# Turning batch 1's query tiles 2 to 4 by DMA, and loading batch 3 behind batch 2's x

## The chip, the core and the metric

The kernel runs on one core of a Trainium2 chip. The metric is device time in microseconds (us), median of several executions. A core has TensorE (PE; PEld is its weight load, which overlaps: 320.1 and 168.3 us busy in the 329.0 us of the kernel before), VectorE (DVE), ScalarE (ACT), GpSimd (POOL) and SyncE (SP), which here only issues DMAs, in the traces one after another (in the changed kernel a load went out at 49.41 us, when the 7.18 us turn before it had ended at 49.31): its "queue". Lines that begin with PE, DVE or the like are views of a profile; L153 is line 153 of the kernel.

## The reference

Linear attention per batch and head, then a gated feed-forward over all 4608 tokens:

```python
# attention: B=8, H=8, S=576, D=64
q_p = phi(q, cos_w, sin_w)       # relu(x)*cos | relu(x)*sin: 128 features
k_p = phi(k, cos_w, sin_w)
kv  = einsum('bhsf,bhsd->bhfd', k_p, v);  z = sum(k_p, axis=2)
x   = einsum('bhsf,bhfd->bhsd', q_p, kv) / (einsum('bhsf,bhf->bhs', q_p, z) + 1e-6)
# feed-forward: 512 -> 1536 -> 512
out = (gelu(x @ w_gate) * (x @ w_val)) @ w_out
```

## The kernel before

Tokens are handled in nine blocks: block 0 is batch 0 (576 tokens), then eight of at most 512. In a block, each of 12 units makes one 128-row slice of the gate and of the value (four matmuls each) and multiplies them. Work for other stages is hung behind units by number: `put(u, ...)` runs behind unit u. Batch b = n+1 gets its attention inside block n: scale q (`sq`) and k (`sk`), cast v, `attn_step` 0 (keys times values), then steps 1 to 5: one 128-query tile each, normalized and turned into `xT`, which later blocks multiply.

Two ways to turn a tile: TensorE transposes into a PSUM bank plus an eviction, or a DMA on SP's queue.

```python
def turn_q(b, j0, j1):                      # by DMA, SP's queue
    nc.sync.dma_start_transpose(out=qT[b % 2][:, j0:j1]..., in_=qp[:, j0:j1]...)

def q_by_pe(b, j, bank, eng, ...):          # by TensorE: 8 transposes, one eviction
    for h in range(h0, h1):
        nc.tensor.transpose(out=qb[:, h, :], in_=qp[:, j, h, :], identity=ident)
    ...
def attn_step(b, i):
    if i == 0:
        kv_half(b, 0, 6); kv_half(b, 1, 7)  # 40 short matmuls, reads kp and vx
    else:
        turn_x(b, i - 1, numer(b, i - 1, 6))    # numerators, normalize, turn x by DMA
# --- batch 1's queries, inside block 0: turned by TensorE
between = { (8, 0): (L(sq, 0, 0, "v"), L(sq, 0, 1, "s")), ...
    (9, 0): (..., L(T, 0, 6, "v")),  (9, 1): (..., L(T, 1, 7, "v")),
    (10, 0): (..., L(T, 2, 6, "v")), (10, 1): (L(load_q, 2), L(T, 3, 7, "v")),
    (11, 0): (L(T, 4, 6, "v"),), ... }
# --- end of batch 1, between output matmuls: batch 2's queries are scaled here
    x_by_pe(1, 0, y[0], 0, "s")
    o_part(0, 2, 4, 8, 12)
    sq(0, 1, "s"), sq(1, 1, "s")
    x_by_pe(1, 1, y[1], 1, "s")
    ...
# --- block 1 differs from later blocks: everything two units (attention: one) earlier
    s = 0 if n > 1 else -2
    put(4 + s, L(cast_v, b, 0, 4), L(cast_v, b, 4, 8, "s"))
    put(5 + (n == 1) + s, L(attn_step, b, 0))
    ...
```

## Time and profile before

| | before |
|---|---|
| time, median | 330.74 us (four runs, 330.67 to 330.81) |
| span of the profiled run | 329.0 us |
| PE busy | 320.1 us |
| VectorE / ScalarE busy | 172.4 / 152.3 us |
| start of block 1, of block 2 | 61.75, 85.79 us |

The page of the kernel before: busy time of each engine with its share and instruction count, and the chain of work that ended last, by engine.

```profile
PE 320.1 (97%) x2247; PEld 168.3 (51%) x2247; DVE 172.4 (52%) x381; ACT 152.3 (46%) x273; POOL 21.4 (7%) x41
...
PE 92%; DMA 3%; DVE 2%; ACT 1%; issue 1%; POOL 0%; SPq 0%; DVEq 0%; POOLq 0%; ACTq 0%
```

TensorE bounds the kernel: a microsecond counts only if it is taken from TensorE's work or from a gap in it. The gaps are few. The view of waits (engine, line, what it waited for: us in total, times, longest):

```profile
PEld L153 <- issue: 2.0, 7, 0.4
...
PE ps L169 <- ACT xT L345: 0.4, 1, 0.4
PE ps L217 <- DMA xT<-xb: 0.3, 1, 0.3
...
PE ps L342 <- DVE xb L184: 0.3, 1, 0.3
```

The last three are at 59.4, 85.8 and 25.4 us. The chain in order of time (start, us, what), one group of query transposes and the stretch before 59.4 us:

```profile
44.04 0.45 PE ps L323 x8
...
57.52 0.28 ACT qp L136
57.80 0.34 issue
58.15 0.71 ACT qp L136
58.85 0.48 ACT xT L345
59.34 0.04 issue
59.38 0.29 PE ps L169 x4
```

Eight transposes hold the chain 0.45 us. Before 59.38 us TensorE stands behind ScalarE: an eviction of x (L345) that queued behind two scalings of the next batch's queries (L136).

### The profile page before, as it was taken

How to read it: one execution, taken by the hardware profiler on the slowest of the kernel's cores; microseconds unless marked ns; L12 is line 12 of the kernel's file. 1: busy time of each engine (PE TensorE's matmuls, PEld its weight loads, DVE VectorE, ACT ScalarE, POOL GpSimd, SP SyncE). 2: the span in 40 equal slices, each digit the busy share in tenths (PEclk: the TensorE clock that was granted, in tenths of full speed). 3: DMA queues.
4: the chain of work that ended last, by engine and by line, in shares of the span. 5: the costliest groups of instructions: out<-in, count | busy, mean ns of one | idle time of the engine just before them, and what ended most of it. 6: DMA issues, size and time to landing. Idle time of an engine off the chain costs nothing.

```text
span 329.0 us, 5914 instructions
## 1 busy us (share of the span) xinstructions
PE 320.1 (97%) x2247; PEld 168.3 (51%) x2247; DVE 172.4 (52%) x381; ACT 152.3 (46%) x273; POOL 21.4 (7%) x41
## 2 busy tenths in 40 slices
PE   7799999999999999999999999999999999999994
PEld 3487876455445444544454445444544444444443
DVE  5895685668654657454835484557545322222210
ACT  6574665872564246523752376227622233222321
POOL 2650010000100010000100010001000100100000
PEclk9999999999999999999999999999999999999999
DMA  7999998799398936996599549974825121000024
GB/s 225 283 205 275 200 364 268 218 223 347 69 170 281 287 65 129 268 286 119 106 272 295 126 88 230 354 115 81 160 48 82 28 52 34 32 32 34 32 65 96
DMA packets 84635, 54.64 MB, mean 166 GB/s; under 512 B 49408, under 2 KB 79872, under 8 KB 84608
## 3 DMA queue, kind: packets, MB, share of 16 engines
q1 hardware_dynamic: 78096, 47.92, 58.8%
q0 software_dynamic: 6080, 5.90, 10.0%
q10 hardware_dynamic: 432, 0.46, 0.4%
q8 instruction: 17, 0.28, 0.3%
q14 instruction: 10, 0.08, 0.1%
HBM read 37.75 MB, written 9.44 MB: 143 GB/s over the span
## 4 chain that ended last, share of the span: by engine, by line
PE 92%; DMA 3%; DVE 2%; ACT 1%; issue 1%; POOL 0%; SPq 0%; DVEq 0%; POOLq 0%; ACTq 0%
PE ps L217 28%; PE ps L228 28%; PE ps L258 27%; PE ps L153 3%; PE ps L169 3%; DMA qf<-in_q_dram 2%; PE ps L323 1%; DMA xT<-xb 1%; PE ps L276 1%; PE ps L342 1%; ACT qp L136 0%; DVE vx L140 0%; DVE xb L184 0%; SPq L79 0%; DVE hT L233 0%
## 5 line engine op out<-in xcount | busy, mean ns | idle before, releaser
L233 DVE TENSOR_TENSOR hT<-gel,ps 128x512 bf16<-128x512 f32 (+5 forms) x126 | 76.3, 610 | 129.4 <-PE ps L228 125.8
L217 PE MATMUL ps<-xT,wg_sb 128*128 128x512 bf16 (+5 forms) x504 | 113.7, 348 | 0.8 <-DMA xT<-xb 0.3
L228 PE MATMUL ps<-xT,wv_sb 128*128 128x512 bf16 (+5 forms) x504 | 113.6, 349 | 0.0
L222 ACT ACTIVATE gel<-ps 128x512 f32<-128x512 f32 (+5 forms) x126 | 67.4, 537 | 78.0 <-PE ps L217 76.7
L258 PE MATMUL ps<-wo_sb,hT 128*128 128x512 bf16 x420 | 96.5, 379 | 0.0
L228 PEld LDWEIGHTS <-wv_sb 128*128 128x128 bf16 x504 | 47.8, 98 | 46.0
L217 PEld LDWEIGHTS <-wg_sb 128*128 128x128 bf16 x504 | 45.6, 98 | 41.1 <-issue 1.6
L258 PEld LDWEIGHTS <-hT 128*128 128x128 bf16 x420 | 40.0, 98 | 45.4
L287 ACT COPY o_sb<-ps 128x512 f32<-128x512 f32 x35 | 20.5, 585 | 74.6 <-PE ps L258 74.6
L184 DVE TENSOR_TENSOR xb<-ps,rec 128x512 bf16<-128x512 f32 (+2 forms) x41 | 27.8, 678 | 2.9 <-DMA xT<-xb 1.5
L136 ACT ACTIVATE kp<-kf,sin_c 128x512 bf16<-128x512 f32 (+1 forms) x41 | 25.4, 682 | 0.8 <-DMA kf<-in_k_dram 0.8
L134 DVE TENSOR_SCALAR qp<-qf,cos_c 128x512 bf16<-128x512 f32 x40 | 19.9, 540 | 0.0
L136 ACT ACTIVATE qp<-qf,sin_c 128x512 bf16<-128x512 f32 x29 | 19.8, 714 | 0.0
L169 PEld LDWEIGHTS <-qT 128*128 128x128 bf16 (+1 forms) x320 | 15.0, 98 | 9.1 <-issue 2.1
L134 DVE TENSOR_SCALAR kp<-kf,cos_c 128x512 bf16<-128x512 f32 (+1 forms) x45 | 18.7, 464 | 1.4 <-DMA kf<-in_k_dram 1.4
L169 PE MATMUL ps<-kv,qT 128*128 128x65 bf16 (+1 forms) x320 | 16.7, 193 | 0.5 <-ACT xT L345 0.4
L208 POOL COPY xT<-xr 128x256 bf16<-128x256 bf16 x6 | 2.7, 443 | 201.8 <-DMA xr<-xb 169.2
L153 PEld LDWEIGHTS <-kp 128*128 128x128 bf16 x320 | 10.8, 97 | 3.3 <-issue 2.0
L126 PE MATMUL ps<-junk 128*128 128x512 bf16 x35 | 10.0, 428 | 1.7 <-DVE par_i L103 1.7
L153 PE MATMUL ps<-vx,kp 128*128 128x65 bf16 x320 | 11.1, 193 | 0.1
L140 ACT CAST vx<-vf 128x1280 bf16<-128x1280 f32 (+1 forms) x9 | 10.2, 1136 | 1.2 <-DMA vf<-in_v_dram 1.2
L244 POOL COPY hT<-hT 128x768 bf16<-128x768 bf16 x8 | 7.6, 945 | 37.9 <-DVE hT L233 37.9
(56 smaller groups left out, 93.2 us busy)
## 6 DMA issues: line engine op xcount, KB each, us to landing
out_dram<-o_sb SPq DMA_DIRECT2D x38, 128.0 KB, 2.4
kf<-in_k_dram SPq DMA_DIRECT2D x7, 640.0 KB, 6.9
out_dram<-o_sb SPq DMA_DIRECT2D x16, 256.0 KB, 2.8
qf<-in_q_dram SPq DMA_DIRECT2D x6, 640.0 KB, 6.0
vf<-in_v_dram SPq DMA_DIRECT2D x6, 640.0 KB, 9.6
kf<-in_k_dram SPq DMA_DIRECT2D x7, 512.0 KB, 5.9
qf<-in_q_dram SPq DMA_DIRECT2D x6, 512.0 KB, 5.0
vf<-in_v_dram SPq DMA_DIRECT2D x6, 512.0 KB, 8.5
```

The costliest lines, as they stand in the source:

```text
L134: nc.vector.tensor_scalar(d, s, col, 0.0, op0=ALU.mult, op1=ALU.max)
L136: nc.scalar.activation(d, s, AF.Relu, scale=col)
L140: cp(vx[b % 2][:, :, h0:h1, 0:D], vf[:, h0:h1].rearrange("p h j d -> p j h d"))
L153: nc.tensor.matmul(ps[:, bank, (h % 4) * (D + 1):(h % 4 + 1) * (D + 1)], lhsT=kp[:, j, h, :], rhs=vx[b % 2][:, j, h, 0:D + 1], start=(j == ...
L169: nc.tensor.matmul(ps[0:rows, bank + g, (h % 4) * (D + 1):(h % 4 + 1) * (D + 1)], lhsT=qT[b % 2][:, t, h, 0:rows], rhs=kv[b % 2][:, h, 0:D ...
L184: nc.vector.tensor_tensor(xb[0:rows, g0:g1], nd[:, :, :, 0:D], rec[0:rows, 0:n, :, None].to_broadcast([rows, n, 4, D]), op=ALU.mult,)
L217: nc.tensor.matmul(ps[:, gb, 0:w], lhsT=wg_sb[:, ct, jt * 128:(jt + 1) * 128], rhs=xT[:, ct, p0:p0 + w], start=(ct == 0), stop=(ct == CT - 1),
L222: nc.scalar.activation(gel[:, 0:w], ps[:, gb, 0:w], AF.Gelu)
L228: nc.tensor.matmul(ps[:, vb, 0:w], lhsT=wv_sb[:, ct, jt * 128:(jt + 1) * 128], rhs=xT[:, ct, p0:p0 + w], start=(ct == 0), stop=(ct == CT - 1),
L233: nc.vector.tensor_mul(hT[n % 2][:, jt, 64 + c0:64 + c0 + w], gel[:, 0:w], ps[:, vb, 0:w])
L258: nc.tensor.matmul(ps[:, bank, :], lhsT=hT[n % 2][:, jt, c0:c0 + 128], rhs=wo_sb[:, jt, :], start=(jt == 0), stop=(jt == JT - 1),)
L287: nc.scalar.copy(o_sb, ps[:, bank, :])
```

## The change

The intent: take 24 transposes from TensorE; free batch 1's end of batch 2's scaling; keep batch 3's loads out of the way of batch 2's x; let block 1 have the same plan as later blocks. The core of the diff:

```diff
-    def x_by_pe(b, t, xb, bank, eng, c0=0, c1=CT):
+    def x_by_pe(b, t, xb, bank, eng, c0=0, c1=CT, every=1):
...
+    gv_unit(0, 1, 384, 128, 5, 7)
     X(4, 0, "v")()
-    gv_unit(0, 1, 384, 128, 5, 7)
+    gv_unit(0, 4, *A, 3, 1)
...
-        (9, 0): (L(sq, 2, 0, "v"), L(sq, 2, 1, "s"), L(T, 0, 6, "v")),
-        ... T 1 to 4 behind (9,1), (10,0), (10,1), (11,0)
+        (8, 0): (L(sq, 2, 0, "v"), L(sq, 2, 1, "s"), L(T, 0, 6, "v"), ),
+        (8, 1): (L(sq, 3, 0, "v"), L(sq, 3, 1, "s"), L(T, 1, 7, "v"), ),
+        (9, 0): (L(sq, 4, 0, "v"), L(sq, 4, 1, "s"), ),
+        (9, 1): (L(turn_q, 1, 2, 5), ),
+        (10, 1): (L(load_q, 2), ),
...
-    sq(0, 1, "s"), sq(1, 1, "s")
     x_by_pe(1, 1, y[1], 1, "s")
...
-    sq(2, 0, "v"), ... turn_q(2, 0, 3) ... turn_q(2, 3, 5)
-    load_q(3)
...                                      # blocks 1 to 6, now without the shift s:
+        put(0, ... sq 0, 1);  put(1, ... sq 2 to 4, turn_q);  put(2, 3, ... sk)
+        put(3, ..., L(cast_v, b, 0, 4))          # was unit 4 (+ s)
+        put(4, L(cast_v, b, 4, 8, "s"))
+        put(5, L(attn_step, b, 0))               # block 1: was unit 4
+            for f, u in zip((load_q, load_k, load_v), (3, 4, 5) if n > 1 else (6, 11, 11)):
+                put(u, L(f, b + 1))
+            put(6 + i, L(attn_step, b, i + 1))   # block 1: was 5 + i
```

In blocks 2 to 6, VectorE's half of the cast of v moves from unit 4 to unit 3 (in block 1, with its shift of two units, from unit 2 to unit 3). Two more edits are not in this cut: tile 4 of batch 1 is now multiplied and turned with 128 rows and not with 64 (`numer(1, 4, 0)`, `every=2`), and of batch 1's v VectorE casts heads 4 and 5 too.

More of the change, by code (lines that the diff above doesn't have):

```diff
@@ L338, in x_by_pe @@
         xb2 = xb.rearrange("p g h d -> p (g h d)")
-        rows = 128 if t < NJ else 64
+        rows = 128 if t < NJ or every == 2 else 64
         view = ps[:, bank, 0:256].bitcast(BF16).rearrange("p (c t) -> p c t", c=CT)
@@ L344, in x_by_pe @@
             )
-        cp(xT[:, c0:c1, p0:p0 + rows], view[:, c0:c1, 0:rows])
+        cp(xT[:, c0:c1, p0:p0 + rows // every], view[:, c0:c1, 0:rows:every])
     def sq(j, which, eng, *h):
@@ L454 @@
     between = {
-        (8, 0): (L(sq, 0, 0, "v"), L(sq, 0, 1, "s")),
-        (8, 1): (L(sq, 1, 0, "v"), L(sq, 1, 1, "s")),
-        (9, 0): (L(sq, 2, 0, "v"), L(sq, 2, 1, "s"), L(T, 0, 6, "v")),
-        (9, 1): (L(sq, 3, 0, "v"), L(sq, 3, 1, "s"), L(T, 1, 7, "v")),
-        (10, 0): (L(sq, 4, 0, "v"), L(sq, 4, 1, "s"), L(T, 2, 6, "v")),
-        (10, 1): (L(load_q, 2), L(T, 3, 7, "v")),
-        (11, 0): (L(T, 4, 6, "v"),),
-        (11, 1): (L(carry, 0),),
+        (7, 0): (L(sq, 0, 0, "v"), L(sq, 0, 1, "s"), ),
+        (7, 1): (L(sq, 1, 0, "v"), L(sq, 1, 1, "s"), ),
+        (8, 0): (L(sq, 2, 0, "v"), L(sq, 2, 1, "s"), L(T, 0, 6, "v"), ),
[3 more added lines that the diff above has]
+        (10, 1): (L(load_q, 2), ),
+        (11, 1): (L(carry, 0), ),
     }
@@ L465 @@
         for i, (c0, w) in enumerate((A, Bw)):
-            gv_unit(0, jt, c0, w, i, 3 - i)
+            if (jt, i) != (4, 0):
+                gv_unit(0, jt, c0, w, i, 3 - i)
             for f in between.get((jt, i), ()):
@@ L476 @@
     cast_v(1, 0, 4, "v")
-    cast_v(1, 4, 8, "s")
+    cast_v(1, 4, 6, "v")
+    cast_v(1, 6, 8, "s")
     load_v(2)
@@ L501 @@
     x_by_pe(1, 2, y[2], 6, "s")
-    y4 = numer(1, 4, 0, 64)
+    y4 = numer(1, 4, 0)
     o_part(0, 3, 5, 5, 10)
     x_by_pe(1, 3, y[3], 7, "s")
-    sq(0, 0, "v"), sq(1, 0, "v")
     o_part(0, 3, 5, 10, 12)
-    x_by_pe(1, 4, y4, 6, "s")
-    sq(2, 0, "v"), sq(2, 1, "s")
-    turn_q(2, 0, 3)
-    sq(3, 0, "v"), sq(3, 1, "s"), sq(4, 0, "v"), sq(4, 1, "s")
-    turn_q(2, 3, 5)
-    load_q(3)
+    x_by_pe(1, 4, y4, 6, "v", every=2)
     def attn_step(b, i):
@@ L529, in put @@
             a[u].extend(fs)
-        if n > 1:
-            put(0, L(sq, 0, 0, "v"), L(sq, 1, 0, "v"), L(sq, 1, 1, "v"), L(sq, 0, 1, "s"))
-            put(1, L(sq, 2, 0, "v"), L(sq, 2, 1, "s"), L(turn_q, b, 0, 3))
-            put(1, L(sq, 3, 0, "v"), L(sq, 4, 0, "v"), L(sq, 4, 1, "v"), L(sq, 3, 1, "s"), L(turn_q, b, 3, 5))
-        s = 0 if n > 1 else -2
-        put(2 + s, L(sk, 0, 0, "v"), L(sk, 1, 0, "v"), L(sk, 0, 1, "s"), L(sk, 1, 1, "s"))
-        put(3 + s, L(sk, 2, 0, "v"), L(sk, 3, 0, "v"), L(sk, 4, 0, "v"))
-        put(3 + s, L(sk, 2, 1, "s"), L(sk, 3, 1, "s"), L(sk, 4, 1, "s"))
-        put(4 + s, L(cast_v, b, 0, 4), L(cast_v, b, 4, 8, "s"))
-        put(5 + (n == 1) + s, L(attn_step, b, 0))
+        put(0, L(sq, 0, 0, "v"), L(sq, 1, 0, "v"), L(sq, 1, 1, "v"), L(sq, 0, 1, "s"))
+        put(1, L(sq, 2, 0, "v"), L(sq, 2, 1, "s"), L(turn_q, b, 0, 3))
+        put(1, L(sq, 3, 0, "v"), L(sq, 4, 0, "v"), L(sq, 4, 1, "v"), L(sq, 3, 1, "s"), L(turn_q, b, 3, 5))
+        put(2, L(sk, 0, 0, "v"), L(sk, 1, 0, "v"), L(sk, 0, 1, "s"), L(sk, 1, 1, "s"))
+        put(3, L(sk, 2, 0, "v"), L(sk, 3, 0, "v"), L(sk, 4, 0, "v"))
+        put(3, L(sk, 2, 1, "s"), L(sk, 3, 1, "s"), L(sk, 4, 1, "s"), L(cast_v, b, 0, 4))
+        put(4, L(cast_v, b, 4, 8, "s"))
+        put(5, L(attn_step, b, 0))
         if b + 1 < B:
-            if n > 1:
-                put(3, L(load_q, b + 1))
-            put(4 + s, L(load_k, b + 1))
-            put(5 + s, L(load_v, b + 1))
+            for f, u in zip((load_q, load_k, load_v), (3, 4, 5) if n > 1 else (6, 11, 11)):
+                put(u, L(f, b + 1))
         for i in range(5):
-            put(6 + (n == 1) + s + i, L(attn_step, b, i + 1))
+            put(6 + i, L(attn_step, b, i + 1))
     for n in range(2, NB):
```

## The prediction

> **What bounds it now.** TensorE: on the page PE is busy 320.1 of 329.0 us, VectorE 52%, ScalarE 46%. The chain that ended last is 92% PE; from 90 us on its PE pieces touch (four 512-column matmuls every 0.86 us). Only PE work taken away, or PE gaps closed, counts. PE's listed waits after the start are short: 0.3 to 0.4 us each at 25.4 (tile 4's x of batch 0), 59.4 (ScalarE's eviction of x) and 85.8 us (DMA of batch 2's x).
>
> **Step 1, query turns of batch 1.** Each group of 8 TensorE transposes holds the chain for 0.45 us (39.65 to 46 us, no PE gap around). Three go: -1.33 us, all critical. VectorE loses three evictions of 0.68 us, worth nothing by themselves. [...] here a 24-block turn took 5.8 us to land. It is off the path if in time: v of batch 1 is issued at 39.5 to 42.2 and lands by 48.6, so the turn should land near 50; its first reader runs near 54. Queries landed by 34.1; first use moves to about 35.
>
> **Step 2, batch 2's query scaling moved from batch 1's end into block 1.** Two ScalarE scalings (0.66 us each) stand before the eviction of x that PE waits for at 59.4. The chain there spends 2.65 us on about 2.1 us of PE work: -0.5 us. Tile 4 with 128 rows costs up to 0.1 us. Later blocks already scale this way without a gap.
>
> **Step 3, start of batch 0.** The 128-column unit put before tile 4's transposes covers the gap at 25.4, but its value needs a bank that VectorE frees at about 25.6: 0.1 us won. With (4, first half) moved ahead, unit (4, second half) follows unit (1, 64 columns) on the same two banks: PE waits for a Gelu, about 0.2 us. Together about +0.1 us.
>
> **Step 4, batch 3's loads behind batch 2's x.** Now 3.5 MB of loads are in flight when batch 2's x is turned: tiles 0 to 3 land in 8.7, 7.0, 5.2, 3.1 us; in quiet blocks 2.4 to 2.5. But attention moves one unit later (about 2 us), and block 2 needs tile 3 at once. From its numerator: 1.9 us to normalized x, 2.5 landing, 0.2 overhead = 4.6 us, against 4.0 us of PE work: a gap of about 0.6 where 0.4 is now, +0.2 us. Keys of batch 3 land an estimated 7.5 to 8.5 us into block 2, needed from 7.6: a short wait, hidden by two banks.
>
> **Total.** -1.33 - 0.5 + 0.1 + 0.1 + 0.2 = about -1.4 us: 329.3 us, range 328.4 to 330.4. Faster by over 2% 0.01, within 2% 0.98, slower 0.01.
>
> **What would show it.** 24 PE transposes fewer and 1.3 us less from 39 to 46 us; no PE wait on the DMA into qT; the PE wait at 59 us gone; a short PE wait on a Gelu near 28 us; a PE wait of 0.3 to 0.9 us on the DMA into xT at block 2's start, tile 3 landing in about 2.5 us; blocks 3 to 8 unchanged to 0.1 us.
>
> **What would make it wrong.** The turn of batch 1's queries landing after its numerators: a stall of some us. Keys or values of batch 3 over 3 us late: a stall in block 2. A later tile 3: up to 1.5 us more. Batch 1's keys or values, now needed 1.4 us earlier, not there yet.

## The result

| | before | after |
|---|---|---|
| time, median (range) | 330.74 us (330.67 to 330.81) | 328.77 us (328.19 to 329.17) |
| span of the profiled run | 329.0 us | 326.8 us |
| PE busy, matmuls | 320.1 us, 2247 | 317.6 us, 2223 |

The ratio is 0.9939 (95% interval 0.9922 to 0.9956): the mean time of one kernel's fast runs over that of the other's of the same rounds, so not quite the ratio of the medians. In us it is -2.0, inside the stated range but 0.6 more gain than the -1.4 predicted.

Where the time went, from the starts of TensorE's matmuls in the two profiles, counted from the first gate matmul. That matmul itself starts between 15.6 and 16.2 us in profiles whose program is the same up to there, so the start is left out.

| stretch | before | after | difference | predicted |
|---|---|---|---|---|
| first gate to first output matmul (block 0) | 30.64 | 29.58 | -1.06 | -1.33 + 0.1 |
| to block 1 (end of batch 1) | 15.02 | 14.29 | -0.73 | -0.5 + 0.1 |
| to block 2 (block 1) | 24.04 | 24.34 | +0.30 | +0.2 |
| to the last matmul (blocks 2 to 8) | 238.75 | 238.20 | -0.55 | 0 |

The 0.1 in the first row is step 3, that in the second row step 2's tile 4 with 128 rows.

The waits of the kernel after, same view:

```profile
PEld L153 <- issue: 0.7, 2, 0.4
...
PE ps L217 <- DMA xT<-xb: 0.8, 1, 0.8
...
PE ps L228 <- DVE hT L233: 0.2, 1, 0.2
...
PE ps L217 <- ACT gel L222: 0.2, 1, 0.2
```

The wait for ScalarE's eviction (L169) is gone. The wait for batch 2's x has grown from 0.3 to 0.8 us. The two 0.2 us waits are new, at 25.2 and 29.6 us, in block 0. And the unnamed wait at L153 fell from 2.0 to 0.7 us.

That last line holds the surprise. The chain, before and then after, in block 2:

```profile
99.76 0.86 PE ps L217 x4
100.62 0.86 PE ps L228 x4
101.49 1.36 PE ps L153 x40
```

```profile
97.95 0.86 PE ps L217 x4
98.81 0.86 PE ps L228 x4
99.67 1.21 PE ps L153 x40
```

The same 40 matmuls hold the chain 0.15 us less, and so they do in each of blocks 2 to 6. VectorE's timeline (start, us, engine, line, operation) around them, before and then after:

```profile
99.87 0.69 DVE L233 TENSOR_TENSOR hT<-gel,ps 128x512 bf16<-128x512 f32 x1 [2.44 <-PE ps L228]
100.47 0.95 DVE L140 CAST vx<-vf 128x1280 bf16<-128x1280 f32 x1
```

```profile
95.53 0.95 DVE L140 CAST vx<-vf 128x1280 bf16<-128x1280 f32 x1
98.05 0.69 DVE L233 TENSOR_TENSOR hT<-gel,ps 128x512 bf16<-128x512 f32 x1 [1.57 <-PE ps L228]
```

Before, the cast of v ended at 101.42 us (100.47 + 0.95), and the matmuls that read it could start only then; after, it ends 3 us ahead of them. That is one theory. The rival, a guess that no view shows: TensorE's program is 24 matmuls shorter, so instruction fetch falls elsewhere; "issue" is the profile's word for a wait without a visible cause.

SP's queue, before and then after, at the turn of batch 1's queries:

```profile
39.46 2.72 SPq L79 DMA_DIRECT2D vf<-in_v_dram  x4
42.34 1.83 SPq L79 DMA_DIRECT2D qf<-in_q_dram  x2
```

```profile
39.41 2.62 SPq L79 DMA_DIRECT2D vf<-in_v_dram  x4
42.13 7.18 SPq L144 DMA_TRANSPOSE qT<-qp  x1
49.41 1.32 SPq L79 DMA_DIRECT2D qf<-in_q_dram  x2
```

The turn holds the queue for 7.18 us, and batch 2's query load goes out 7 us later than before. Inside the whole change nobody needs those queries until block 1.

### The profile page after: what moved, and what is told of

It is laid out like the page before. It is cut to its first block, busy times and chain, and to the rows that moved or that the text cites. A ratio compares the mean times of both kernels' runs of the same rounds, so it can differ in the third digit from the quotient of the medians.

```text
span 326.8 us, 5867 instructions
## 1 busy us (share of the span) xinstructions
PE 317.6 (97%) x2223; PEld 167.0 (51%) x2223; DVE 171.8 (53%) x382; ACT 150.6 (46%) x270; POOL 21.2 (6%) x41
## 4 chain that ended last, share of the span: by engine, by line
PE 93%; DMA 3%; DVE 1%; ACT 1%; issue 1%; POOL 0%; SPq 0%; DVEq 0%; POOLq 0%; ACTq 0%
PE ps L217 28%; PE ps L228 28%; PE ps L258 28%; PE ps L169 3%; PE ps L153 3%; DMA qf<-in_q_dram 2%; PE ps L323 1%; DMA xT<-xb 1%; PE ps L342 1%; PE ps L276 1%; DVE vx L140 0%; SPq L79 0%; DVE hT L233 0%; DVE qT L331 0%; DVE xb L184 0%
## 5 line engine op out<-in xcount | busy, mean ns | idle before, releaser
L169 PEld LDWEIGHTS <-qT 128*128 128x128 bf16 (+1 forms) x320 | 15.0, 98 | 8.7 <-issue 1.9
L136 ACT ACTIVATE qp<-qf,sin_c 128x512 bf16<-128x512 f32 x27 | 18.5, 712 | 0.0
L169 PE MATMUL ps<-kv,qT 128*128 128x65 bf16 (+1 forms) x320 | 16.5, 193 | 0.2
L153 PEld LDWEIGHTS <-kp 128*128 128x128 bf16 x320 | 10.9, 97 | 2.6 <-issue 0.7
L153 PE MATMUL ps<-vx,kp 128*128 128x65 bf16 x320 | 11.1, 193 | 0.1
```

The source lines that it names most:

```text
L136: nc.scalar.activation(d, s, AF.Relu, scale=col)
L153: nc.tensor.matmul(ps[:, bank, (h % 4) * (D + 1):(h % 4 + 1) * (D + 1)], lhsT=kp[:, j, h, :], rhs=vx[b % 2][:, j, h, 0:D + 1], start=(j == ...
L169: nc.tensor.matmul(ps[0:rows, bank + g, (h % 4) * (D + 1):(h % 4 + 1) * (D + 1)], lhsT=qT[b % 2][:, t, h, 0:rows], rhs=kv[b % 2][:, h, 0:D ...
```

## The experiments

Twelve kernels ran; all gave the correct result. Each was timed beside the kernel before on its chip.

| run | us, median | before there | ratio |
|---|---|---|---|
| cast_only | 329.94 | 330.58 | 0.9984 |
| turn_only | 333.82 | 330.58 | 1.0092 |
| act_only | 330.18 | 330.58 | 0.9986 |
| after_rep | 328.81 | 330.58 | 0.9948 |
| turn_back | 330.13 | 331.04 | 0.9977 |
| cast_back | 330.06 | 331.04 | 0.9979 |
| x_pe | 328.35 | 331.04 | 0.9924 |
| loads_early | 334.08 | 331.04 | 1.0105 |
| q_first | 335.07 | 330.63 | 1.0124 |
| bank_free | 328.66 | 330.63 | 0.9933 |
| best1 | 327.95 | 330.63 | 0.9918 |
| best2 | 327.52 | 330.63 | 0.9904 |

### The cast of v: cast_only and cast_back

To the kernel before (cast_only):

```diff
-        put(4 + s, L(cast_v, b, 0, 4), L(cast_v, b, 4, 8, "s"))
+        put((3 if n > 1 else 4) + s, L(cast_v, b, 0, 4))
+        put(4 + s, L(cast_v, b, 4, 8, "s"))
```

> The kernel before with one line moved: in blocks 2 to 6 VectorE casts heads 0 to 3 of v after unit 3 and not after unit 4. TensorE's program is not changed by a single instruction. Theory (the cast ended 0.05 us before the keys-times-values matmuls could start, so they started 0.15 us late in five blocks): the 0.37 us between the last value matmul and the second weight load of those matmuls falls to 0.22 us in blocks 2 to 6 and the time falls by 5 x 0.15 = 0.77 us, to about 330.0. Rival (the 0.15 us per block is instruction fetch, and left because TensorE's program is 48 instructions shorter): nothing changes, 330.7.

Measured: -0.64 us by the medians, -0.53 us by the ratio (95% interval -0.96 to -0.13). In the profile the time from the last value matmul to the second weight load of the 40 is 0.37 us before and 0.22 us here, in all five blocks, and from block 2 to the last matmul the program takes 238.00 us against 238.75: five times 0.15. The chain in block 2, to be held against the 1.36 us of the kernel before:

```profile
101.21 1.21 PE ps L153 x40
```

TensorE's program is unchanged, so the rival falls.

The reverse, to the changed kernel (cast_back):

```diff
-        put(3, ..., L(cast_v, b, 0, 4))
-        put(4, L(cast_v, b, 4, 8, "s"))
+        put(3, ...)
+        put(4, L(cast_v, b, 0, 4), L(cast_v, b, 4, 8, "s"))
```

> The changed kernel with VectorE's cast of v heads 0 to 3 after unit 4 again in blocks 1 to 6; nothing else. Theory: +0.15 us in each of five or six blocks, +0.8 us, about 329.6, and the 0.37 us before the second weight load of the keys-times-values matmuls is back. Rival (that gap came from where TensorE's program is fetched): no change, 0.22 us stays.

Measured: 330.06 us; against the changed kernel, by the ratios to before (0.9979 here), +1.0 to +1.3 us (0.9948 or 0.9939), with two chips between them. The profile shows the mechanism more sharply than the times: 0.37 us is back in five blocks, and from block 2 to the last matmul the program takes 238.95 us against 238.20 in the changed kernel, +0.75 = 5 x 0.15. In block 1 the first of the matmuls came 0.47 us later than with the early cast, but block 2's wait for x was 0.4 us shorter in exchange.

### The turn by DMA: turn_only, turn_back, q_first

turn_only is the kernel before with the new table `between` and tile 4 of batch 1 turned with 128 rows (`every=2`), nothing else.

> The kernel before with query tiles 2 to 4 of batch 1 turned by DMA (queries scaled one unit pair earlier, tile 4's x turned with 128 rows), nothing else. Theory: 24 transposes of TensorE are gone, 3 x 0.445 = 1.33 us on the path, and the next stage is still TensorE's: about 329.4. Rival (the next stage is held by ScalarE and VectorE, whose casts of v end just before the keys-times-values matmuls, so part of the gain turns into a wait there): 0.3 to 0.8 us less gain, 329.7 to 330.2, with a gap before the first of those matmuls.

Measured: 333.82 us, 3.2 us slower than before. Both expectations missed the time. Their first step held: block 0 is 1.35 us shorter than before. The stretches behind it lost more: 1.0 us at the end of batch 1, 1.9 us in block 1, 1.9 us in blocks 2 to 8 (by the profiled run, one of the slower ones). The two matmuls that ended a wait in its TensorE timeline there, and SP's and ScalarE's side of the first:

```profile
58.89 0.29 PE L169 MATMUL ps<-kv,qT 128*128 128x65 bf16 x4 [1.59 <-ACT xT L345]
87.12 1.04 PE L217 MATMUL ps<-xT,wg_sb 128*128 128x512 bf16 x4 [2.28 <-DMA xT<-xb]
```

```profile
42.01 6.53 SPq L144 DMA_TRANSPOSE qT<-qp  x1
48.63 1.32 SPq L79 DMA_DIRECT2D qf<-in_q_dram  x2
...
57.04 1.33 ACT L136 ACTIVATE qp<-qf,sin_c 128x512 bf16<-128x512 f32 x2 [1.02 <-DMA qf<-in_q_dram]
58.27 1.05 ACT L345 COPY xT<-ps 128x512 bf16<-128x512 bf16 x2
```

Batch 2's queries landed at 57 us, because their load stood behind the turn. ScalarE waited for them, the eviction of x waited for ScalarE, and TensorE for the eviction: 1.59 us. A second wait of 2.28 us came at block 2's start. There is a third loss behind it, in the chain:

```profile
87.12 1.04 PE ps L217 x4
88.16 1.48 PE ps L228 x4
```

Four matmuls that take 0.86 us in the kernel before took 1.48: TensorE's clock was granted at half for 3.41 us from 88.27 us on (a mean of 0.78 from 86 to 90 us and of 0.79 from 90 to 94). In the six executions the mean clock of the span was 0.993 to 0.995 in the four slowest (333.48 to 335.12 us) and 1.000 in the two fastest (331.81 and 332.28).

The fall came after the wait: TensorE had been idle for 2.28 us up to 87.12 us and at work again for 1.15 us when the clock fell at 88.27. In q_first below, the granted clock was 0.77 from 86 to 90 us and 0.81 from 90 to 94, after a wait of 2.01 us; in loads_early, with a wait of 4.56 us, it was at half for 6.83 us (a mean of 0.51 and 0.64 in the same two windows). In the changed kernel, with its wait of 0.85 us, it was 1.00 from 75 to 325 us. What sets the fall off was not tested.

The opposite experiment turns tiles 2 to 4 on TensorE again within the changed kernel (turn_back):

```diff
-        (9, 0): (..., L(sq, 4, 1, "s"), ),
-        (9, 1): (L(turn_q, 1, 2, 5), ),
+        (9, 0): (..., L(sq, 4, 1, "s"), L(T, 2, 6, "v"), ),
+        (9, 1): (L(T, 3, 7, "v"), ),
+        (10, 0): (L(T, 4, 6, "v"), ),
...
-    y4 = numer(1, 4, 0)
+    y4 = numer(1, 4, 0, 64)
...
-    x_by_pe(1, 4, y4, 6, "v", every=2)
+    x_by_pe(1, 4, y4, 6, "v")
```

> The changed kernel with query tiles 2 to 4 of batch 1 turned by TensorE again; the rest of the change stays. Theory (inside the whole change the DMA turn is free, because batch 2's queries, whose load stands behind it in the DMA queue for 7 us, are no longer needed before block 1): +1.33 us, about 330.1, with the stretch from unit (7,0) to the first output matmul 1.33 us longer. Rival (the DMA turn also costs something inside the whole change, through the late query load): under 0.9 us more.

Measured: 330.13 us, +1.0 to +1.3 us over the changed kernel by the ratios, whose job was another. In the profile block 0 is 1.36 us longer, as the theory says; block 2's wait for x is 0.42 us instead of 0.85, so a part comes back, as the rival says. From the first gate to the last matmul it is +1.25 us. That includes 0.22 us at the end of batch 1 from tile 4, which this run turns with 64 rows again (see act_only). So the same turn is worth 1.0 to 1.3 us inside the change, while turn_only lost 3.2 us with it. One thing that differs is who needs the queries that stand behind it: that accounts for the loss at the end of batch 1, not for the larger one from block 2's start on.

q_first tests the loss at the end of batch 1 by order: turn_only with the query load ahead of the turn.

```diff
-        (9, 1): (L(turn_q, 1, 2, 5), ),
-        (10, 1): (L(load_q, 2), ),
+        (9, 1): (L(load_q, 2), L(turn_q, 1, 2, 5), ),
```

> The kernel before with batch 1's query tiles 2 to 4 turned by DMA, as in the run turn_only (333.8 us), but with the load of batch 2's queries issued ahead of that turn and not behind it. Theory (turn_only lost because the turn holds the DMA queue 6.5 us and batch 2's queries then land at 57 us, after ScalarE wants them): the queries land by about 50, the 1.6 us wait of TensorE for ScalarE's eviction falls back to 0.35 us or less, and the time is at least 1.2 us below turn_only: 330 to 332.5, lower if the wait at block 2's start (2.3 us there) goes too. Rival (the turn itself, or its lateness for tiles 2 to 4, is what costs): a wait on the DMA into qT appears and the time stays near 333.8.

Measured: 335.07 us, no better, as the rival says. Its TensorE waits after block 0:

```profile
55.24 0.43 PE L169 MATMUL ps<-kv,qT 128*128 128x65 bf16 x8 [1.38 <-DMA qT<-qp]
59.13 0.29 PE L169 MATMUL ps<-kv,qT 128*128 128x65 bf16 x4 [0.47 <-ACT xT L345]
87.10 1.04 PE L217 MATMUL ps<-xT,wg_sb 128*128 128x512 bf16 x4 [2.01 <-DMA xT<-xb]
```

The mechanism of the theory held: with the queries in time, the wait for ScalarE fell from 1.59 to 0.47 us. But its time did not: the turn now landed 11.6 us after its issue and was itself waited for, 1.38 us. In neither order were both in time. With the early need for the queries taken away, as in the change, the turn fits; other ways were not tried.

The wait at block 2's start stayed at 2.0 to 2.3 us in both kernels. The lateness of batch 3's loads does not look like the cause: their query load left SP's queue at 69.6 to 69.9 us, where it left at 69.0 before, but the last of them landed at 83.6 to 83.7 us, as before (83.75). Tiles 1 to 3 of x landed 1.4 us later than before all the same. The DMA packets in the traces show a candidate that no run tested. The page lists a queue q8, "instruction" (17 packets, 0.28 MB in the kernel before); one 16 KB transfer on it ran from 83.6 to 84.8 us in turn_only and from 84.0 to 85.1 in q_first, where it ran from 79.5 to 80.6 before. Then the DMA all but stopped while three turns of x were under way, in turn_only (the last two figures are DMA share and GB/s):

```profile
84.30:85.50 1.20, 0.55 (x3) 0.05 (x1) 1.20 (x3) 0.32 (x1) 0.00 (x0) 1.00 0.06 6
```

The changed kernel shows the same in small: of its first three turns of batch 2's x two landed in 2.5 to 2.7 us, and the third, into which such a transfer fell (80.1 to 81.5 us), in 4.2.

### The scaling behind the eviction: act_only

To the kernel before:

```diff
-    sq(0, 1, "s"), sq(1, 1, "s")
     x_by_pe(1, 1, y[1], 1, "s")
...
     x_by_pe(1, 2, y[2], 6, "s")
+    sq(0, 1, "s"), sq(1, 1, "s")
```

> The kernel before with the two ScalarE scalings of batch 2's queries tiles 0 and 1 put behind the eviction of x of tile 2 and not before that of tile 1; nothing else. Theory: the eviction of tile 1 is no longer behind 1.3 us of scaling, TensorE's wait at 59.4 us is gone: -0.6 us, 330.1. Rival (the wait only moves to the eviction of tile 3, which then stands behind the same scalings): under 0.2 us of gain.

Measured: -0.40 us by the medians, -0.46 by the ratio (95% interval -0.89 to -0.03). The wait at 59.4 us is gone from the profile, and block 1 starts 0.51 us earlier, counted from the first gate. The rival falls. The change gets 0.73 us in this stretch, and the profiles tell where the other 0.22 us come from: tile 4 of batch 1 with 128 rows. turn_back, which has the 64 rows and everything else of this stretch as the change, takes 14.51 us for it, as act_only does, against 14.29. Tile 4's eight numerators in the chain, here (64 rows) and in the changed kernel (128 rows):

```profile
58.77 0.37 PE ps L169 x8
```

```profile
57.40 0.26 PE ps L169 x8
```

The other half of the 0.22 us lies around the tile's four transposes. The prediction had booked the 128 rows as a cost of up to 0.1 us.

### The loads behind batch 2's x: loads_early

To the changed kernel:

```diff
-            for f, u in zip((load_q, load_k, load_v), (3, 4, 5) if n > 1 else (6, 11, 11)):
+            for f, u in zip((load_q, load_k, load_v), (3, 4, 5)):
```

> The changed kernel with batch 3's loads where all later blocks have them (q, k, v after units 3, 4, 5 of block 1) and not behind batch 2's x. Theory (loads in flight slow the turns of x): tile 0's turn lands in 5 us or more instead of 2.5, tile 3's later too, and block 2's wait grows from 0.9 us by 0.5 to 1.2 us: 329.3 to 330.0. Rival (the loads are over by the time tile 3 is turned; the wait is the turn's own latency): no change, within 0.2 us.

Measured: 334.08 us, about 5.3 us slower than the changed kernel (328.81) by the medians of two jobs; the direction was right, the size not. From issue to landing (min, median, max) of the four turns of x by DMA, in the changed kernel and in this one:

```profile
DMA to landing us min/median/max: 2.5/2.8/4.2
```

```profile
DMA to landing us min/median/max: 4.8/6.7/10.1
```

SP's queue backed up behind the first turns, tile 3 was issued at 83.0 us and took 4.8 us, and TensorE stood still. Timeline, chain, and a window with the granted clock (after the engines' busy times: clock, DMA share, GB/s):

```profile
87.85 1.89 PE L217 MATMUL ps<-xT,wg_sb 128*128 128x512 bf16 x4 [4.56 <-DMA xT<-xb]
...
87.85 1.89 PE ps L217 x4
89.73 1.71 PE ps L228 x4
...
86.00:90.00 4.00, 2.15 (x6) 0.78 (x7) 1.28 (x2) 0.23 (x1) 0.38 (x2) 0.51 0.55 104
```

The wait is 4.56 us against 0.85, and then four matmuls take 1.89 and 1.71 us, about twice the 1.02 and 0.86 us of the kernel before, at a granted clock of 0.51. So putting batch 3's loads behind batch 2's x is not a nicety: without it the change would lose 3 us to the kernel before. How much of the 4.56 us is the loads alone was not separated: an instruction transfer of 16 KB ran here too, from 83.3 to 84.9 us, amid the turns. That moving the attention one unit later needs the loads' new place, and the moved scaling the later attention, is argued, not tested.

### The rest: x_pe, bank_free, best1, best2, after_rep

x_pe takes the remaining wait of block 2 (0.85 us) by turning one tile of x on TensorE, whose transposes fit behind the next tile's numerators:

```diff
+        elif (b, i) == (2, 4):
+            held.append(numer(b, 3, 6))
         else:
             turn_x(b, i - 1, numer(b, i - 1, 6))
+            if (b, i) == (2, 5):
+                x_by_pe(2, 3, held[0], 4, "s")
```

> The changed kernel with tile 3 of batch 2's x turned by four TensorE transposes and a ScalarE eviction instead of a DMA; nothing else. Theory (the 0.85 to 0.98 us in which block 2's first matmul waits is the latency of that one tile's DMA): the wait goes, 0.22 us of transposes come: -0.6 to -0.75 us, about 328.1. Rival (tile 2's DMA, or the DMA queue in general, is as late): the wait shrinks by less than 0.4 us, 328.6 or more.

Measured: 328.35 us, ratio 0.9924 against 0.9939 and 0.9948 of the changed kernel, so -0.5 to -0.8 us. The wait is gone; the transposes hold the chain 0.22 us. The theory holds.

bank_free changes the banks of one unit in block 0:

```diff
-                gv_unit(0, jt, c0, w, i, 3 - i)
+                gv_unit(0, jt, c0, w, *((4, 6) if (jt, i) == (4, 1) else (i, 3 - i)))
```

> The changed kernel with unit (4, second half) of batch 0 on banks 4 and 6 and not on banks 1 and 2, which the unit before it has just filled; nothing else. Theory (TensorE waits 0.20 us for that unit's Gelu): the wait at 29.6 us goes, -0.2 us, 328.6. Rival (the wait moves to the next unit): no change.

Measured: 328.66 us. The times can't tell 0.2 us apart. In the profile the wait for the Gelu is gone and block 0 is 0.37 us shorter than in the changed kernel.

best1 joins x_pe and bank_free:

> The changed kernel with tile 3 of batch 2's x turned by TensorE (as x_pe, 328.35) and unit (4, second half) on free banks (as bank_free). Theory: the two gains add, 328.1 to 328.2, and TensorE has no listed wait over 0.3 us after 26 us. Rival: one of them hides the other, 328.35 or more.

Measured: 327.95 us. The gains add, and in the same job it is 0.7 us below bank_free.

best2 adds to best1:

```diff
-    gv_unit(0, 1, 384, 128, 5, 7)
-    X(4, 0, "v")()
-    gv_unit(0, 4, *A, 3, 1)
+    gv_unit(0, 4, *A, 1, 3)
+    X(4, 0, "s")()
+    gv_unit(0, 1, 384, 128, 5, 7)
```

> best1 with unit (4, first half) put ahead of tile 4's transposes and of the 128-column unit, and tile 4 evicted by ScalarE. Theory: the longer unit (0.87 us) covers the wait for tile 4's normalized x and for VectorE's bank at 25.2 us: another -0.25 us, about 327.9. Rival (its value weights, which landed only near 25.5 us in the kernel before, are now waited for): a wait on the DMA into wv_sb and no gain.

Measured: 327.52 us, the fastest of all: ratio 0.9904 to the kernel before. No wait on the weights appears, and the wait at 25.2 us is gone. By the two ratios it is about 1.1 to 1.5 us faster than the changed kernel.

after_rep is the changed kernel again:

> The changed kernel once more, unchanged. Its four runs spread over 1.0 us (328.2 to 329.2) where the kernel before spreads over 0.14. Theory: a wait for a DMA at the start of block 2 varies between executions: again a spread of about 1 us, and the wait on the DMA into xT in the profile differs from 0.85 us. Rival: the first job's spread was chance, and runs now agree within 0.2 us.

Measured: 328.81 us, 328.46 to 329.21; the wait on the DMA into xT was 0.98 us. But the kernel before spread as much on this chip (330.12 to 331.12), so the narrow 0.14 us of its first runs says nothing special; neither the theory of the varying wait nor an agreement within 0.2 us is borne out.

## Why the prediction was right or wrong

The total was right, 328.77 us in a range of 328.4 to 330.4, with 0.6 us more gain than the point. That it came so near the range's lower end is owed to gains that the prediction did not have, the cast of v (0.75 us) and tile 4's rows (0.22 us), against a little less than predicted in blocks 0 and 1. Point by point:

- **What bounds it: right.** Every effect found is TensorE work or a TensorE gap.
- **Step 1, -1.33 us on the path: right inside the change** (turn_back: block 0 1.36 us longer). The turn landed at 51.4 us (42.13 + 9.3), where "near 50" was predicted, ahead of its reader at 54.1. But the step's list of risks missed the one that turn_only showed: the turn holds SP's queue 7.18 us and delays what stands behind it. The prediction treated the four steps as a sum. They are not: without step 2, TensorE stood 1.59 us for the late queries (turn_only) or 1.38 us for the late turn (q_first).
- **Step 2, -0.5 + 0.1: the -0.5 right, the 0.1, the author's estimate, wrong in sign.** act_only shows the named wait and -0.51 us. Tile 4 with 128 rows saved 0.22 us where up to 0.1 was booked as its cost; together they are the stretch's -0.73.
- **Step 3, "together about +0.1 us": right in mechanism, too small.** Both predicted waits are in the profile (0.24 us for VectorE's bank, 0.20 us for the Gelu). Block 0's -1.06 us is 0.27 us short of step 1's -1.33; bank_free took 0.37 us back.
- **Step 4, a gap of about 0.6 where 0.4 was: right**, 0.85 to 0.98 us, in the stated 0.3 to 0.9 or just above. Batch 3's keys, estimated at 7.5 to 8.5 us into block 2, landed 6.3 us into it (90.3 us) and were first read 7.6 us into it (91.57 us), without a wait. loads_early shows what it never asked: what the loads' place was worth, 5.3 us, with the instruction transfer not separated.
- **"blocks 3 to 8 unchanged to 0.1 us": wrong.** Blocks 2 to 8 took 0.55 us less. The prediction read the last hunk as a plan for block 1 and did not see that the cast of v moves in blocks 2 to 6 too; of the 2.0 us that the waits put down to "issue" at L153, 1.4 lie in these blocks, five times 0.27, and 0.15 of each was the wait for that cast. Five times 0.15 us is more than the 0.6 us by which the point fell short; a new wait of 0.19 us in block 3 gave some of it back.

## What to carry to other kernels

Work moved to a DMA queue costs the queue's time as well as its own: ask what stands behind it in the same queue, and who needs that first. Here a turn of 24 blocks of 128x128 held SP's queue for 7.18 us with loads in flight and for 3.83 us in block 1 of the kernel before, against 0.6 us for one load of 512 KB. It landed in 9.3 us and in 5.8 us, 0.39 and 0.24 us a block, where eight transposes on TensorE hold the chain for 0.45 us, 0.056 us each.

Parts of a change that enable one another can't be costed as a sum. A wait that the profile calls "issue" and that repeats in every block deserves a look at what ends just before it, here a VectorE cast that cost 0.15 us a block.

A stall cost more than its length here: after waits of 2.28 us (turn_only) and 2.01 us (q_first) TensorE's clock was at half for 3.41 us in the profiled runs, and the mean clock was 0.992 to 0.995 in four of six and four of five executions. After the changed kernel's 0.85 us it stayed at 1.00.

Before a late DMA is put down to the loads beside it, look whether an instruction transfer fell into it: in the changed kernel a turn of x with one beside it landed in 4.2 us, the two before it in 2.5 to 2.7. That the one holds up the other is the author's guess; no run here tested it.
